# Loading, weight and summing order in a channel-gate kernel: a shorter lead load, a two-part first gate, and 16 rows of each tile summed on VectorE

## The chip, the cores and the metric

One core of one Trainium2 chip runs the program. The metric is the device time of one execution in microseconds (us). The kernel before took 528.62 us, the median of three runs (528.31 to 529.32). A profile's span, from the first to the last instruction, is about 1.5 us shorter than that time.

## The reference

```python
def reference(x, w1d):                      # x: 1 x 384 x 384 x 384 bf16, w1d: one bf16
    B, H, W, C = x.shape
    g = jnp.einsum("bhwc->bc", x) / (H * W)  # mean of every channel
    s = _sigmoid(g * w1d[0])                 # (cut: with k = 1 the padded loop is this product)
    return x * s[:, None, None, :]
```

Every element must be read once and written once, 113.25 MB each way. Only 384 channel sums stand between.

## The kernel before

The data are 1,152 rows of 128 partitions x 384 channels. Twelve rows are the lead, then 19 tiles of 60 rows follow through four slots of SBUF. The kernel guesses the gate from the first 4 rows (`s_early` in the code), multiplies each tile by that guess (VectorE; in place, but for the last tile, which goes to a free slot) and stores it. Meanwhile it sums all rows: TensorE 52 rows of each tile, VectorE 8. At the end it computes the true gate and compares the two bit by bit; if they differ, a second pass does everything again. On this input they agree, so the second pass never runs.

```python
FIRST, EARLY, TILE, SLOTS, BOTH, OWN, PAUSE = 12, 4, 60, 4, 3, 8, 8
...
    load(base, FIRST, 0)                                     # SyncE: the lead
    for k in range(BOTH):
        load(slot(k), TILE, row0(k), ("sync", "scalar"))     # half a tile on each queue
        if k == 0:
            plan.dma("scalar", w_one[0:1, 0:1], w1d.unsqueeze(0), writes=["w_one"])
    for k in range(BOTH, SLOTS):
        load(slot(k), TILE, row0(k))                         # tile 3: SyncE alone
...
    for k in range(n_tiles):
        if k >= SLOTS:
            for i in range(2) if k == SLOTS else () if k < SLOTS + 2 else (k - SLOTS,):
                sum_own(i)                                   # VectorE: 8 rows
                put(slot(i), TILE, row0(i))                  # gate in place, store on ScalarE
            if k == SLOTS:
                pause(slot(k))                               # ScalarE, after store 0 has landed
            load(slot(k), TILE, row0(k), reads=["pause"] if k == SLOTS else ())
...
    put(slot(last), TILE, row0(last), slot(n_tiles))         # last tile: gate, then own sum
    sum_own(last)
    put(base, FIRST, 0)
    join_own()                                               # then the true gate and the check
```

Because the gate works in place, it must wait until TensorE has read the rows. The load of tile k waits until the store of tile k - 4 has landed.

Of the kernel before, what the change touches and what calls it, by code (L numbers as in the profile page):

```python
# [149 lines left out]
def split(n, most):  # L150
    k = -(-n // most)
    return [n // k + (i < n % k) for i in range(k)]
# [3 lines left out]




FIRST, EARLY, TILE, SLOTS, BOTH, OWN, PAUSE = 12, 4, 60, 4, 3, 8, 8  # L160


def bass_standalone__channel_attn_eca__vision_kernel(
# [5 lines left out]
    B, H, W, C = x.shape  # L169
# [4 lines left out]
    def dram(view, r0, n):  # L174
        return view[r0 * P : (r0 + n) * P, :].rearrange("(p t) c -> p (t c)", p=P)

    ones = nc.alloc_sbuf_tensor("ones", [P, P], BF16)
    s_early = nc.alloc_sbuf_tensor("s_early", [P, C], BF16)
    w_one = nc.alloc_sbuf_tensor("w_one", [1, 16], BF16)
# [17 lines left out]
    def at(r0, n):  # L197
        assert r0 + n <= n_arena
        return arena[:, r0 * C : (r0 + n) * C]

    def rows(r0, n):
        return [("sb", r) for r in range(r0, r0 + n)]

    def gate(to, place, n, s):
        s_b = s[:].unsqueeze(1).broadcast_to([P, n, C])
        v, to_v = (at(r, n).rearrange("p (t c) -> p t c", t=n) for r in (place, to))
        return lambda e: e.tensor_tensor(to_v, v, s_b, ALU.mult)  # L207

    n_tiles = (n_rows - FIRST) // TILE
    base = SLOTS * TILE  # L210
# [3 lines left out]
    ready = nc.alloc_semaphore("ready")  # L214

    def slot(k):
        return k % SLOTS * TILE

    def row0(k):
        return FIRST + k * TILE  # L220
# [2 lines left out]
    s_true = at(base + FIRST, 1)  # L223
    plan = Planner(nc, "a", 70)

    def load(place, n, r0, queues=("sync",), reads=()):
        i = 0
        for queue, m in zip(queues, split(n, -(-n // len(queues)))):
            plan.dma(
                queue,  # L230
                at(place + i, m),
                dram(x_rows, r0, n)[:, i * C : (i + m) * C],
                reads=reads,
                writes=rows(place + i, m),
            )
            i += m
# [3 lines left out]
    def mm(e, bank, weights, moving, start, stop):  # L240
        if not loaded:
            loaded.append(e.matmul(bank, weights, moving, start=start, stop=stop))  # L242
            return loaded[0]
        return e.add_instruction(  # L244
            mybir.InstMatmult(
                name=nc.get_next_instruction_name(),
                engine=mybir.EngineType.PE,
                ins=[e.lower_ap(moving), e.lower_ap(weights)],
                outs=[e.lower_ap(bank)],
                start_tensor_calc=start,  # L250
                stop_tensor_calc=stop,
                ldweights=False,
            )
        )

    def add_rows(e, group, column, n, start, stop):

        n_wide = n * C // WIDE
        all_of = [
            mm(  # L260
                e,
                acc[group][i % 3][:, :],
                ones[:],
                arena[:, column + i * WIDE : column + (i + 1) * WIDE],
                start and i < 3,
                stop and i >= n_wide - 3,
            )
            for i in range(n_wide)
        ]
        return all_of[-1]  # L270
# [9 lines left out]
    def sum_others():  # L280

        def one(e, s):
            e.wait_ge(ready, 1).then_inc(ready, -1)  # L283
            add_rows(e, 1, slot(s) * C, TILE - OWN, False, False).then_inc(
                plan.sems["tensor"], 1
            )

        def emit(e):
            add_rows(e, 1, (base + EARLY) * C, 4, True, False)
            rounds = -(-n_tiles // SLOTS)  # L290
            some = n_tiles - (rounds - 1) * SLOTS
            with e.Fori(0, rounds) as k:
                for s in range(some):
                    one(e, s)
                if some < SLOTS:
                    with e.If(k < rounds - 1):
                        for s in range(some, SLOTS):
                            one(e, s)
            add_rows(
                e, 1, (base + EARLY + 4) * C, FIRST - EARLY - 4, False, True  # L300
            ).then_inc(plan.sems["tensor"], 1)

        plan.streams["tensor"].append(("block", emit, None))
# [16 lines left out]
    def sum_own(k):  # L320

        r0 = slot(k) + TILE - OWN
        view = at(r0, OWN).rearrange("p (t c) -> p c t", t=OWN)
        to = part if k else own
        plan.op(
            "vector",
            lambda e: e.reduce_sum(to[:], view, axis=mybir.AxisListType.X),  # L327
            reads=rows(r0, OWN),
            writes=["part" if k else "own"],
        )  # L330
        if k:
            plan.op(
                "vector",
                lambda e: e.tensor_tensor(own[:], own[:], part[:], ALU.add),  # L334
                reads=["own", "part"],
                writes=["own"],
            )
# [34 lines left out]
            writes=["total"],  # L372
        )

    def put(place, n, r0, to=None):
        to = place if to is None else to
        plan.op(
            "vector",
            gate(to, place, n, s_early),
            reads=["s_early"] + rows(place, n),  # L380
            writes=rows(to, n),
        )
        plan.final.append(
            plan.dma("scalar", dram(o_rows, r0, n), at(to, n), reads=rows(to, n))
        )

    def pause(r0):

        to = at(base + FIRST + 1, PAUSE)
        plan.op(  # L390
            "scalar",
            lambda e: e.activation(  # L392
                to, warm[:, 0:1].broadcast_to([P, PAUSE * C]), ACT_F.Sigmoid
            ),
            reads=["warm"],
            writes=rows(r0, 1) + ["pause"],
        )
# [26 lines left out]

    plan.op("gpsimd", lambda e: e.memset(warm[:, 0:1], 0.0), writes=["warm"])
    plan.op("vector", lambda e: e.memset(ones[:], 1.0), writes=["ones"])  # L426
    load(base, FIRST, 0)
    for k in range(BOTH):
        load(slot(k), TILE, row0(k), ("sync", "scalar"))
        if k == 0:  # L430
            plan.dma("scalar", w_one[0:1, 0:1], w1d.unsqueeze(0), writes=["w_one"])
    for k in range(BOTH, SLOTS):
        load(slot(k), TILE, row0(k))
    heads = {e: len(plan.streams[e]) for e in ("sync", "scalar")}
    weight()
    sum_first()
# [6 lines left out]
        reads=["total", "w_scaled0", "warm1"],  # L443
        writes=["s_early"],
    )
    plan.need("tensor", rows(base, FIRST))
    sum_others()

    for k in range(n_tiles):
        if k >= SLOTS:  # L450

            for i in range(2) if k == SLOTS else () if k < SLOTS + 2 else (k - SLOTS,):
                sum_own(i)
                put(slot(i), TILE, row0(i))
            if k == SLOTS:
                pause(slot(k))
            load(slot(k), TILE, row0(k), reads=["pause"] if k == SLOTS else ())
        there = rows(slot(k), TILE)
        plan.relay(ready, "gpsimd", "tensor", there, there, ["acc1"])
    plan.signals("tensor", rows(base, FIRST), ["acc1"])  # L460
    for k in range(n_tiles - SLOTS, last):
        sum_own(k)
        put(slot(k), TILE, row0(k))

    put(slot(last), TILE, row0(last), slot(n_tiles))
    sum_own(last)
    put(base, FIRST, 0)
# [9 lines left out]
        reads=["total", "w_scaled1"],  # L477
        writes=["s_true"],
# [6 lines left out]
        reads=["s_true", "s_early"],  # L485
        writes=["total"],
# [4 lines left out]
        reads=["total"],  # L491
        writes=["wrong"],
# [4 lines left out]
        reads=["wrong"],  # L497
        writes=["redo"],
# [5 lines left out]
    half, r0 = base // 2, 0  # L504
    for k, n in enumerate(split(n_rows, half)):
        place = k % 2 * half
# [4 lines left out]
            reads=rows(place, n),  # L511
            writes=rows(place, n),
# [9 lines left out]
    def ahead(name, e, n):  # L522




        block = nc.main_func.blocks[0].instructions
        at_end = len(block)
        plan.emit(name, e, n)
        new = block[at_end:]  # L530
        del block[at_end:]
        barrier = next(
            i
            for i, ins in enumerate(block)
            if ins.engine == e.engine and isinstance(ins, mybir.InstDrain)
        )
        block[barrier:barrier] = new

    ahead("sync", nc.sync, 1)
    ahead("scalar", nc.scalar, 1)  # L540
    plan.emit("sync", nc.sync, heads["sync"] - 1)
    plan.emit("scalar", nc.scalar, heads["scalar"] - 1)

    with nc.Block() as block:
# [66 lines left out]
```

## Time and profile before

| | before |
|---|---|
| time, median of 3 | 528.62 us |
| span of the profiled run | 527.0 us |
| bytes through the DMA engines | 226.51 MB |
| weight's matmul starts | 15.31 us |
| first tile's sum starts on TensorE | 24.18 us |
| first store issued / landed | 47.64 / 74.3 us |
| check ends / last store lands | 518.1 / 526.9 us |

VectorE idled for 73.6 us before its gates, waiting for TensorE. This is what the change goes at. No engine but the DMA engines is near its limit.

### The profile page before, as it was taken

The page shows a single profiled execution, that of the slowest core. Times are in us where ns is not written, and L with a number is a line of the kernel's source. Part 1 is how long each engine was busy: PE and PEld are TensorE (multiplying, and loading weights), DVE is VectorE, ACT ScalarE, POOL GpSimd, SP SyncE. Part 2 cuts the span into 40 slices and gives each one's busy share as a digit, 9 for nine tenths or more (in the row PEclk, how much of TensorE's full clock was granted, in tenths as well). Part 3 has the DMA queues.
Part 4 walks back from the last instruction along what each step waited for, and adds up shares of the span by engine and source line. Part 5 has one row for each costly group of instructions (what it writes and reads, how often), then busy time and mean ns, then how long its engine had stood idle before and what let it go on. Part 6 is the DMA issues. An engine that isn't in the chain of part 4 may idle for free. (4 is left out here: it accounts for less than half of the span.)

```text
span 527.0 us, 1015 instructions
## 1 busy us (share of the span) xinstructions
PE 198.5 (38%) x754; PEld 0.2 (0%) x2; DVE 353.9 (67%) x81; ACT 5.5 (1%) x5; POOL 0.3 (0%) x5
## 2 busy tenths in 40 slices
PE   0389170070706151524333342516060707070810
PEld 0000000000000000000000000000000000000000
DVE  0639999649494858576666666666666666758892
ACT  1000020000000000000000000000000000000000
POOL 0000000000000000000000000000000000000000
PEclk9999766576767667675758585858585858585765
DMA  9999999999999999999999999999999999999998
GB/s 383 434 421 418 448 448 395 444 448 448 395 444 448 448 395 444 448 444 399 444 448 444 399 444 448 445 399 444 444 444 406 441 444 444 406 441 444 444 406 363
DMA packets 6196, 226.51 MB, mean 430 GB/s; under 512 B 690, under 2 KB 690, under 8 KB 690
## 3 DMA queue, kind: packets, MB, share of 16 engines
q10 hardware_dynamic: 3314, 122.10, 53.6%
q1 hardware_dynamic: 2880, 104.40, 46.1%
q14 instruction: 2, 0.02, 0.0%
HBM read 113.25 MB, written 113.25 MB: 430 GB/s over the span
## 5 line engine op out<-in xcount | busy, mean ns | idle before, releaser
L244 PE MATMUL acc<-arena,ones 128*128 128x512 bf16 x749 | 196.6, 429 | 288.4 <-PEq L283 288.4
L207 DVE TENSOR_TENSOR arena<-arena,s_early 128x23040 bf16<-128x23040 bf16 (+1 forms) x20 | 233.5, 11677 | 78.0 <-PE acc L244 73.6
L327 DVE TENSOR_REDUCE part<-arena 128x384 f32<-128x3072 bf16 x18 | 96.4, 5355 | 67.3 <-DMA arena<-in_x_dram 67.3
L334 DVE TENSOR_TENSOR own<-own,part 128x384 f32<-128x384 f32 x18 | 10.0, 558 | 0.6
L418 DVE TENSOR_SCALAR w_scaled<-w_all 128x1 f32<-128x1 f32 x2 | 0.2, 152 | 14.3 <-PE w_all L409 14.3
L409 PE MATMUL w_all<-w_one,ones 1*128 1x1 bf16 x1 | 0.2, 158 | 15.3 <-DMA w_one<-in_w1d_dram 15.3
L244 PE MATMUL acc_own<-terms,ones 128*128 128x384 bf16 x3 | 1.4, 479 | 10.5 <-DVE terms L345 10.5
L327 DVE TENSOR_REDUCE own<-arena 128x384 f32<-128x3072 bf16 x1 | 5.3, 5305 | 0.0
L474 ACT ACTIVATE arena<-total,w_scaled 128x384 bf16<-128x384 f32 x1 | 0.6, 615 | 439.0 <-DVE total L315 439.0
L315 DVE TENSOR_TENSOR total<-total,acc 128x128 f32<-128x128 f32 (+2 forms) x11 | 4.5, 408 | 0.4
L392 ACT ACTIVATE arena<-warm 128x3072 bf16<-128x3072 f32 x1 | 2.8, 2763 | 54.1 <-DMA out_dram<-arena 54.1
L313 DVE COPY total<-acc 128x384 f32<-128x384 f32 x1 | 0.6, 558 | 1.2 <-PE acc L244 1.2
L403 ACT ACT_TABLE_LOAD x1 | 1.3, 1283 | 2.3 <-issue 2.3
L352 DVE TENSOR_TENSOR own<-own,terms 128x384 f32<-128x384 f32 x2 | 1.1, 558 | 0.1
L345 DVE CAST terms<-own 128x384 bf16<-128x384 f32 x3 | 1.1, 357 | 0.1
L482 DVE TENSOR_TENSOR total<-arena,s_early 128x384 f32<-128x384 uint16 x1 | 0.6, 557 | 0.7 <-ACT arena L474 0.7
L370 DVE TENSOR_TENSOR total<-total,acc_own 128x384 f32<-128x384 f32 x1 | 0.6, 554 | 0.6 <-PE acc_own L244 0.6
L426 DVE MEMSET ones<- 128x128 bf16 x1 | 0.2, 165 | 1.0 <-PEq L596 1.0
L440 ACT ACTIVATE s_early<-total,w_scaled 128x384 bf16<-128x384 f32 x1 | 0.6, 615 | 15.8 <-DVE total L315 15.8
L242 PE MATMUL acc<-arena,ones 128*128 128x512 bf16 x1 | 0.6, 608 | 0.0
L490 DVE TENSOR_REDUCE wrong<-total 128x1 f32<-128x384 f32 x1 | 0.6, 552 | 0.0
L403 ACT ACTIVATE warm<-warm 128x1 f32<-128x1 f32 x1 | 0.2, 203 | 0.0
(8 smaller groups left out, 0.9 us busy)
## 6 DMA issues: line engine op xcount, KB each, us to landing
out_dram<-arena ACTq DMA_DIRECT2D x19, 5760.0 KB, 47.4
arena<-in_x_dram SPq DMA_DIRECT2D x16, 5760.0 KB, 38.9
arena<-in_x_dram ACTq DMA_DIRECT2D x3, 2880.0 KB, 27.4
arena<-in_x_dram SPq DMA_DIRECT2D x3, 2880.0 KB, 36.4
arena<-in_x_dram SPq DMA_DIRECT2D x1, 1152.0 KB, 10.3
out_dram<-arena ACTq DMA_DIRECT2D x1, 1152.0 KB, 16.9
w_one<-in_w1d_dram ACTq DMA_DIRECT2D x1, 0.0 KB
```

What stands on the lines that cost most here:

```text
L207: return lambda e: e.tensor_tensor(to_v, v, s_b, ALU.mult)
L242: loaded.append(e.matmul(bank, weights, moving, start=start, stop=stop))
L244: return e.add_instruction(mybir.InstMatmult(name=nc.get_next_instruction_name(), engine=mybir.EngineType.PE, ins=[e.lower_ap(moving), e.l ...
L313: emit = lambda e, part=part, of=of: e.tensor_copy(part, of)
L315: emit = lambda e, part=part, of=of: e.tensor_tensor(part, part, of, ALU.add)
L327: lambda e: e.reduce_sum(to[:], view, axis=mybir.AxisListType.X),
L334: lambda e: e.tensor_tensor(own[:], own[:], part[:], ALU.add),
L345: lambda e, term=term: e.tensor_copy(term, own[:]),
L352: lambda e, term=term: e.tensor_tensor(own[:], own[:], term, ALU.subtract),
L370: lambda e: e.tensor_tensor(total[:], total[:], acc_own[:, :C], ALU.add),
L392: lambda e: e.activation(to, warm[:, 0:1].broadcast_to([P, PAUSE * C]), ACT_F.Sigmoid),
L403: lambda e: e.activation(warm[:, 1:2], warm[:, 0:1], ACT_F.Sigmoid),
```

## The change

Its intent is to make the first store earlier and to take TensorE's sum out of the gate's way. The lead is cut to 8 rows and the other 4 go to ScalarE's queue. The weight goes right behind the lead on SyncE's queue. The first tile is gated in two parts, of which the first needs only the first 32 rows summed. VectorE sums 16 rows of each tile in place of 8, TensorE 44 in place of 52. The pause on ScalarE becomes 9 rows long in place of 8.

```diff
-FIRST, EARLY, TILE, SLOTS, BOTH, OWN, PAUSE = 12, 4, 60, 4, 3, 8, 8
+FIRST, EARLY, TILE, SLOTS, BOTH, FORE, OWN = 12, 4, 60, 4, 3, 32, 16
+PAUSE = 9
...
-            add_rows(e, 1, slot(s) * C, TILE - OWN, False, False).then_inc(
-                plan.sems["tensor"], 1
-            )
+            for r, n in ((0, FORE), (FORE, TILE - OWN - FORE)):
+                add_rows(e, 1, (slot(s) + r) * C, n, False, False).then_inc(
+                    plan.sems["tensor"], 1
+                )
...
-    load(base, FIRST, 0)
-    for k in range(BOTH):
-        load(slot(k), TILE, row0(k), ("sync", "scalar"))
+    LEAD = EARLY + 4
+    load(base, FIRST, 0, hi=LEAD)
+    plan.dma("sync", w_one[0:1, 0:1], w1d.unsqueeze(0), writes=["w_one"])
+    for k in range(SLOTS):
+        load(slot(k), TILE, row0(k), ("sync", "scalar") if k < BOTH else ("sync",))
         if k == 0:
-            plan.dma("scalar", w_one[0:1, 0:1], w1d.unsqueeze(0), writes=["w_one"])
-    for k in range(BOTH, SLOTS):
-        load(slot(k), TILE, row0(k))
+            load(base, FIRST, 0, ("scalar",), lo=LEAD)
...
-                put(slot(i), TILE, row0(i))
+                put(slot(i), TILE, row0(i), parts=None if i else (FORE, TILE - FORE))
```

(Cut: `put` gates part by part, `load` takes a range of rows, the semaphores that tell of TensorE's parts, and the queue heads.)

More of the change, by code (lines that the diff above doesn't have):

```diff
@@ L224, in bass_standalone__channel_attn_eca__vision_kernel, with load @@
     plan = Planner(nc, "a", 70)
-    def load(place, n, r0, queues=("sync",), reads=()):
-        i = 0
-        for queue, m in zip(queues, split(n, -(-n // len(queues)))):
+    def load(place, n, r0, queues=("sync",), lo=0, hi=None, reads=()):
+        i, hi = lo, hi or n
+        for queue, m in zip(queues, split(hi - lo, -(-(hi - lo) // len(queues)))):
             plan.dma(
@@ L373, in join_own, with put @@
         )
-    def put(place, n, r0, to=None):
-        to = place if to is None else to
-        plan.op(
-            "vector",
-            gate(to, place, n, s_early),
-            reads=["s_early"] + rows(place, n),
-            writes=rows(to, n),
-        )
+    def put(place, n, r0, to=None, parts=None):
+        to, i = place if to is None else to, 0
+        for m in parts or [n]:
+            plan.op(
+                "vector",
+                gate(to + i, place + i, m, s_early),
+                reads=["s_early"] + rows(place + i, m),
+                writes=rows(to + i, m),
+            )
+            i += m
         plan.final.append(
@@ L445, in bass_standalone__channel_attn_eca__vision_kernel @@
     )
-    plan.need("tensor", rows(base, FIRST))
+    plan.need("tensor", rows(base, LEAD))
     sum_others()
@@ L457, in bass_standalone__channel_attn_eca__vision_kernel @@
             load(slot(k), TILE, row0(k), reads=["pause"] if k == SLOTS else ())
-        there = rows(slot(k), TILE)
-        plan.relay(ready, "gpsimd", "tensor", there, there, ["acc1"])
+        there = rows(slot(k), TILE) + (rows(base + LEAD, FIRST - LEAD) if k == 1 else [])
+        plan.relay(ready, "gpsimd", "tensor", there, rows(slot(k), FORE), ["acc1"])
+        plan.signals("tensor", rows(slot(k) + FORE, TILE - OWN - FORE), ["acc1"])
     plan.signals("tensor", rows(base, FIRST), ["acc1"])
@@ L537, in ahead @@
         block[barrier:barrier] = new
-    ahead("sync", nc.sync, 1)
+    ahead("sync", nc.sync, 2)
     ahead("scalar", nc.scalar, 1)
-    plan.emit("sync", nc.sync, heads["sync"] - 1)
+    plan.emit("sync", nc.sync, heads["sync"] - 2)
     plan.emit("scalar", nc.scalar, heads["scalar"] - 1)
```

## The prediction

> **What bounds the kernel now.** I read the page's slices first, then the windows, then the timeline of both ends, and last the waits of the DMA queues. The slices and the packet totals:
>
> ```profile
> DMA  9999999999999999999999999999999999999998
> GB/s 383 434 421 418 448 448 395 444 448 448 395 444 448 448 395 444 448 444 399 444 448 444 399 444 448 445 399 444 444 444 406 441 444 444 406 441 444 444 406 363
> DMA packets 6196, 226.51 MB, mean 430 GB/s; under 512 B 690, under 2 KB 690, under 8 KB 690
> ```
>
> The DMA engines are busy in every slice; VectorE is at 67% and TensorE at 38% of the span. The swing between 395 and 448 GB/s is no real swing: a slice counts a packet whole, and most packets are 46,080 bytes. Windows as long as one tile's period show it. The columns are the window, its length, busy time of PE, PEld, DVE, ACT and POOL, the granted clock, DMA share and GB/s:
>
> ```profile
> 408.00:435.20 27.20, 10.33 (x39) 0.00 (x0) 18.08 (x4) 0.00 (x0) 0.00 (x0) 0.69 1.00 434
> 435.20:462.40 27.20, 10.41 (x39) 0.00 (x0) 18.09 (x4) 0.00 (x0) 0.00 (x0) 0.69 1.00 434
> 462.40:489.50 27.10, 10.47 (x39) 0.00 (x0) 18.05 (x3) 0.00 (x0) 0.00 (x0) 0.69 1.01 435
> ```
>
> So the steady stage runs at 434 GB/s, with VectorE busy for 18.1 of 27.2 us. One row of the kernel is 128 x 384 x 2 = 98,304 bytes, which at 434 GB/s is 0.2265 us, or 4.415 rows per us. A tile is 60 rows in and 60 out, 27.2 us: the period is the traffic, nothing else. All 226.51 MB at 434 GB/s take 521.9 us. The span is 527.0 us, so only 5.1 us lie outside full-rate transfer, and no change that keeps the bytes can take more than that.
>
> I looked for those 5.1 us in the packet records, spreading each packet's bytes evenly over its own time. About 1.7 us are gone before the transfers are up to speed (first packet at 1.0 us). From 2 to 50 us, with loads alone, the rate is 430 to 433, which costs 0.4 us more. Between 50.6 and 53.5 us each of the 16 engines has one 46,080-byte load packet of about 2.6 us in place of 1.7 us, just ahead of the first store's first packet: 0.9 us. The steady stage adds 0.6 us of drift. The rest, some 1.5 us, is the tail: most engines finish their last data at 525.1 to 525.5, one at 526.46, and the final wait ends at 527.0.
>
> The head, with the work that the change touches:
>
> ```profile
> 15.31 0.16 PE L409 MATMUL w_all<-w_one,ones 1*128 1x1 bf16 x1 [15.31 <-DMA w_one<-in_w1d_dram]
> 19.52 5.30 DVE L327 TENSOR_REDUCE own<-arena 128x384 f32<-128x3072 bf16 x1
> 24.18 11.17 PE L244 MATMUL acc<-arena,ones 128*128 128x512 bf16 x39 [6.04 <-PEq L283]
> 35.45 12.16 DVE L207 TENSOR_TENSOR arena<-arena,s_early 128x23040 bf16<-128x23040 bf16 x1 [10.63 <-PE acc L244]
> 47.64 18.36 ACTq L109 DMA_DIRECT2D out_dram<-arena  x2
> ```
>
> The weight lands at 15.2, the first tile at 24.0, its TensorE sum ends at 35.4 and holds the gate, and the first store goes out at 47.64. That looks like a long latency, but 252 rows of loads need 252 x 0.2265 = 57 us, so the DMA engines have work throughout it. The queue's own waits and the issues say the same of the rest:
>
> ```profile
> SPq L109 <- DMA out_dram<-arena: 368.8, 14, 26.9
> out_dram<-arena ACTq DMA_DIRECT2D x19, 5760.0 KB, 47.4
> arena<-in_x_dram SPq DMA_DIRECT2D x16, 5760.0 KB, 38.9
> ```
>
> A store is in flight for 47.4 us and a load for 38.9 us, against a period of 27.2: on average 1.7 stores and 1.4 loads stand in the queues, and a load is never late for the engines, only for its slot.
>
> **What the Trainium skill says.** "DMA: Bandwidth & Descriptors", Specifications, gives a fabric ceiling of 435 GB/s; the 434 of the steady windows is that ceiling to within rounding. The same page, Queues, rings and completion order, says each engine takes packets in turn from the rings that have work. The trace agrees: in the head, packets of q1 (SyncE) and q10 (ScalarE) alternate one for one on each engine, so a small packet costs the other ring nearly nothing, and a transfer's landing depends on what it alternates with. "VectorE: DVE Perf Modes", the perf-mode tier table, lists tensor_reduce at one element per cycle only. The trace has 3,072 elements in 5.36 us, 1.74 ns each, even slower, so the page bounds this cost only from below. "TensorE: Matmul & The Clock Gate", Part 1, gives half clock until some microseconds of activity have passed; in the trace the first tile's matmuls start 427 ns apart for 13 of them and then 216 ns apart.
>
> **The change, part by part.** *Lead of 8 rows.* Its 8 packets per engine are 6,144 bytes in place of 9,216. ScalarE's first packets start only at 2.7 us, so about 6 of the 8 pass alone and the lead lands near 6 us (10.3 before). *Weight on SyncE.* It is next on that ring, one or two turns of 0.85 us later: about 7.6 us (15.2 before). From the weight to s_early took 20.24 - 15.31 = 4.9 us, so s_early stands at about 12.5. *Rows 8 to 11 on ScalarE.* While SyncE's half of tile 0 moves, its partner packets are partly these 3,072-byte ones, not 23,040-byte ones of tile 1. In total 8 + 60 + about 4 rows precede the landing: 72 x 0.2265 = 16.3, plus the 1.9 us of start, so about 18 us (24.0 before).
>
> *VectorE 16 rows.* The reduce is 6,144 elements: 10.7 us if time goes with the elements, about 8.5 us if part of the 5.36 us belongs to each of the 384 outputs (one cycle per element plus 5.2 cycles an output). I take 10.7 to be safe. In the first tile it starts when ScalarE's half lands, about 14.5, and ends by 25. *TensorE 44 rows.* 33 matmuls a tile in place of 39. The first 32 rows are 24 matmuls: 13 x 0.427 + 11 x 0.216 = 7.9 us, so from 18.2 to 26.1. *Gate in two parts.* 12.16 us for 60 rows is 0.203 us a row: 6.5 us for 32 rows, 5.7 us for 28, together 12.2 with almost no added cost. It begins at 26.1 and ends at 38.3. The first store goes out at about 38.5, 9 us earlier.
>
> What these 9 us buy is little. At 38.5 ScalarE's ring still has loads until about 42, so the store queues behind them and starts then, not at 53. Store 0 lands at about 70 (74 before), then the pause (9 rows: 9/8 x 2.76 = 3.1 us), and load 4 goes out at about 73 (77 before). VectorE then needs 10.7 + 0.56 + 12.16 = 23.4 us a tile (18.1 before): stores 1, 2 and 3 at about 62, 85 and 108 (65.7, 83.5, 101.4 before). They are needed where the store before them ends, about 70, 92 and 120. Both rings stay filled, and 23.4 is under 27.2. The ceiling is the same.
>
> At the end, the own sum of the last tile adds 5.3 us to the path of the last store and of the check, less the 4 us by which the loads run earlier:
>
> ```profile
> 510.01 0.34 ACTq L109 DMA_DIRECT2D out_dram<-arena  x1
> 517.94 0.15 DVE L496 CAST redo<-wrong 128x1 int32<-128x1 f32 x1
> ```
>
> The last store would be issued at about 511.5 and is needed when the 60 rows before it are through, about 523. The check would end near 519.5 and its flag is read in 1.8 us; the stores end at about 525. Both stay hidden.
>
> The sum: traffic 521.9 unchanged; start 1.7 unchanged; read-only drift shorter by about 0.1; the 0.9 us pause of the engines before the first store gone or not, I give it 50%, so 0.45; tail unchanged. 528.62 - 0.1 - 0.45 is 528.1 us.
>
> **The rivals.** *First: the pause before the first store goes away wholly.* It may come from ScalarE's ring starting again after it ran dry at 41; in the changed kernel it does not run dry. For it: no such gap is seen where a ring stays filled. Against: SyncE's ring runs dry at 69 and starts again at 77 without a loss, so it may belong to the first write to HBM, which remains. If it goes: 527.6. *Second: VectorE becomes the bound.* This needs a 16-row reduce over 27.2 - 12.7 = 14.5 us, 2.4 ns an element. Nothing in the trace speaks for it; 18 reduces lie within 5.29 to 5.43 us. If it came, 1 us over would cost about 15 us: 540 and more. *Third: a ring runs dry* in the head, because stores 2 and 3 come 2 to 7 us later than before, or at the end. My margins are 7 to 12 us; a miss would cost 1 to 3 us: 530. *Fourth: the latency is worth its face value*, 9 us, 519. The windows contradict it, as 521.9 is the floor.
>
> **Range and chances.** Rivals one and four bound it from below at about 527; repeats before spread from 528.31 to 529.32, and a short dry ring costs about 1. So 526.9 to 529.2. Over 2% faster would be below 518, under the floor: 1%. Over 2% slower needs the second rival: 2%.
>
> **What would show it.** Right: weight matmul near 8, first tile's matmuls near 18, gates of 6.5 and 5.7 us, first store near 38.5, reduces of 8.5 to 10.7 us, 434 GB/s in a steady window. The pause shows in the packets just before the first store. Wrong: VectorE without idle time before its reduces in the steady stage, or a window of a tile's length under 430 GB/s.

## More of the kernel before

The slices, the steady windows, both ends of the timeline and the queue's waits stand in the prediction. Two more views are needed for the comparison. These are the page's line of busy time by engine, two groups of instructions (line, engine, operation, tiles and shapes, count, then busy us and mean ns, then idle time before them), and one DMA issue line (count, size, us to landing):

```profile
PE 198.5 (38%) x754; PEld 0.2 (0%) x2; DVE 353.9 (67%) x81; ACT 5.5 (1%) x5; POOL 0.3 (0%) x5
...
L207 DVE TENSOR_TENSOR arena<-arena,s_early 128x23040 bf16<-128x23040 bf16 (+1 forms) x20 | 233.5, 11677 | 78.0 <-PE acc L244 73.6
L327 DVE TENSOR_REDUCE part<-arena 128x384 f32<-128x3072 bf16 x18 | 96.4, 5355 | 67.3 <-DMA arena<-in_x_dram 67.3
...
arena<-in_x_dram ACTq DMA_DIRECT2D x3, 2880.0 KB, 27.4
```

## The result

The changed kernel took 528.29 us, the median of 6 runs (528.18 to 528.51); in the same rounds the kernel before took 529.16 us in its 6 (528.31 to 530.3). The ratio is 0.9984, with a 95% interval of 0.9971 to 0.9997. Ratios here are the mean time of one kernel's runs over that of the other's runs of the same rounds, so not quite the ratio of the medians.

The slices and packets of the changed kernel, then its windows of a tile's period (columns as in the prediction):

```profile
DMA  9999999999999999999999999999999999999998
GB/s 387 430 422 460 406 448 395 444 448 448 395 444 448 448 395 444 448 441 402 444 448 434 409 445 444 434 413 441 448 430 416 441 444 434 416 441 444 430 420 367
DMA packets 6340, 226.51 MB, mean 430 GB/s; under 512 B 706, under 2 KB 706, under 8 KB 962
```

```profile
408.00:435.20 27.20, 9.10 (x33) 0.00 (x0) 23.18 (x3) 0.00 (x0) 0.00 (x0) 0.69 1.00 434
435.20:462.40 27.20, 9.17 (x33) 0.00 (x0) 23.18 (x3) 0.00 (x0) 0.00 (x0) 0.69 1.00 434
```

The bytes and the rate are the same to the last digit that is shown. VectorE went from 18.1 to 23.2 us of a 27.2 us period, and the rate did not change. The page's busy line, the two groups and the DMA issues say where its work went:

```profile
PE 178.2 (34%) x640; PEld 0.2 (0%) x2; DVE 451.1 (86%) x82; ACT 5.8 (1%) x5; POOL 0.3 (0%) x5
...
L209 DVE TENSOR_TENSOR arena<-arena,s_early 128x23040 bf16<-128x23040 bf16 (+3 forms) x21 | 233.5, 11123 | 5.2 <-DMA arena<-in_x_dram 4.0
L331 DVE TENSOR_REDUCE part<-arena 128x384 f32<-128x6144 bf16 x18 | 189.5, 10526 | 53.4 <-DMA arena<-in_x_dram 53.4
...
out_dram<-arena ACTq DMA_DIRECT2D x19, 5760.0 KB, 44.7
arena<-in_x_dram SPq DMA_DIRECT2D x16, 5760.0 KB, 40.9
arena<-in_x_dram ACTq DMA_DIRECT2D x3, 2880.0 KB, 34.5
```

The gates' wait for TensorE fell from 73.6 us to nearly none, and the reduces doubled in its place. ScalarE's three half-tile loads take 34.5 us to land (the median, so the middle one), not 27.4. That line turns out to matter. The head of the changed kernel's timeline:

```profile
9.18 0.16 PE L415 MATMUL w_all<-w_one,ones 1*128 1x1 bf16 x1 [9.18 <-DMA w_one<-in_w1d_dram]
...
14.56 10.49 DVE L331 TENSOR_REDUCE own<-arena 128x384 f32<-128x6144 bf16 x1 [1.08 <-DMA arena<-in_x_dram]
...
26.31 12.23 DVE L209 TENSOR_TENSOR arena<-arena,s_early 128x12288 bf16<-128x12288 bf16 x2 [1.26 <-PE acc L247]
...
38.57 23.45 ACTq L109 DMA_DIRECT2D out_dram<-arena  x2
...
74.23 3.08 ACT L398 ACTIVATE arena<-warm 128x3456 bf16<-128x3456 f32 x1 [60.11 <-DMA out_dram<-arena]
```

The first store is issued at 38.57 us, 9.1 us earlier than before. But the pause behind its landing starts at 74.23, where it started at 74.31 before: the whole 9 us were lost in the queue. In the packet records, ScalarE's ring (its queue on each of the 16 DMA engines) still carries loads. Their last packet ends at 51.0 us and the load lands at 53.2 us. The first store's first packet starts at 51.3 us on one engine and at 54.7 to 55.2 on the others. Before, it came at 53.1 to 53.5. So load 4 is issued at 77.34 (77.10 before), and from there on the two kernels run the same course. The tail:

```profile
502.05 10.41 DVE L331 TENSOR_REDUCE part<-arena 128x384 f32<-128x6144 bf16 x1
...
515.55 0.34 ACTq L109 DMA_DIRECT2D out_dram<-arena  x1
...
523.48 0.15 DVE L503 CAST redo<-wrong 128x1 int32<-128x1 f32 x1
```

The check ends at 523.6 us, 5.5 us later than before. ScalarE then reads the flag and passes its waits for the stores; it is through all but the last at 526.07 us, and the last store lands at 526.67. The room between the two was 6 us before (waits through at 520.8, last landing at 526.9) and is down to 0.6 us.

### The profile page after: what moved, and what is told of

The parts are those of the page before. It is cut to its first block, busy times and chain, and to the rows that moved or that the text cites. A ratio compares the mean times of both kernels' runs of the same rounds, so it can differ in the third digit from the quotient of the medians. Undisturbed runs are those within 1.5% of the kernel's fastest.

```text
span 526.7 us, 905 instructions
## 1 busy us (share of the span) xinstructions
PE 178.2 (34%) x640; PEld 0.2 (0%) x2; DVE 451.1 (86%) x82; ACT 5.8 (1%) x5; POOL 0.3 (0%) x5
## 4 chain that ended last, share of the span: by engine, by line
DMA 64%; DVE 27%; issue 4%; PE 2%; ACT 0%; DVEq 0%
DMA out_dram<-arena 33%; DMA arena<-in_x_dram 31%; DVE arena L209 13%; DVE part L331 12%; PE acc L247 1%; DVE own L338 1%; DVE total L319 0%; DVE own L356 0%; DVE terms L349 0%; ACT arena L481 0%; DVE total L489 0%; DVE total L374 0%; DVE wrong L497 0%; PE acc_own L247 0%; DVE redo L503 0%
## 5 line engine op out<-in xcount | busy, mean ns | idle before, releaser
L247 PE MATMUL acc<-arena,ones 128*128 128x512 bf16 x635 | 176.3, 447 | 314.0 <-PEq L286 314.0
L209 DVE TENSOR_TENSOR arena<-arena,s_early 128x23040 bf16<-128x23040 bf16 (+3 forms) x21 | 233.5, 11123 | 5.2 <-DMA arena<-in_x_dram 4.0
L331 DVE TENSOR_REDUCE part<-arena 128x384 f32<-128x6144 bf16 x18 | 189.5, 10526 | 53.4 <-DMA arena<-in_x_dram 53.4
L331 DVE TENSOR_REDUCE own<-arena 128x384 f32<-128x6144 bf16 x1 | 10.5, 10495 | 1.1 <-DMA arena<-in_x_dram 1.1
L398 ACT ACTIVATE arena<-warm 128x3456 bf16<-128x3456 f32 x1 | 3.1, 3082 | 60.1 <-DMA out_dram<-arena 60.1
L245 PE MATMUL acc<-arena,ones 128*128 128x512 bf16 x1 | 0.6, 608 | 0.0
## 6 DMA issues: line engine op xcount, KB each, us to landing
arena<-in_x_dram ACTq DMA_DIRECT2D x3, 2880.0 KB, 34.5
```

The costliest lines, as they stand in the source:

```text
L209: return lambda e: e.tensor_tensor(to_v, v, s_b, ALU.mult)
L245: loaded.append(e.matmul(bank, weights, moving, start=start, stop=stop))
L247: return e.add_instruction(mybir.InstMatmult(name=nc.get_next_instruction_name(), engine=mybir.EngineType.PE, ins=[e.lower_ap(moving), e.l ...
L331: lambda e: e.reduce_sum(to[:], view, axis=mybir.AxisListType.X),
L398: lambda e: e.activation(to, warm[:, 0:1].broadcast_to([P, PAUSE * C]), ACT_F.Sigmoid),
```

## The experiments

The questions are these. Is the difference of 0.16% real, and which part makes it? What are the 0.9 us before the first store? How close are the two other bounds, the tail and VectorE? And where do the long runs of the kernel before come from? Twelve runs were made, all with correct results.

### Before against itself, the change again, and its halves

These four ran on one chip in the same rounds, five of them. The first is unchanged:

> The kernel before, unchanged, timed against itself. Both theories: ratio 1.000; the width of the interval says how small a difference can be believed. If the spread of the first six runs (528.31 to 530.3) is of the kernel, its runs should again spread over 1 to 2 us, and its profile should show one DMA engine ending 1 us or more after the others.

The change again:

> The changed kernel again. Theory A (the transfers alone set the time, the change moves only what lies under them): within 0.5 us of before in the median, ratio 0.998 to 1.000. Theory B (the earlier first store buys real time): ratio below 0.9975, and the gain shows as bytes moved earlier in the head, which the first profile does not have (the lag behind full rate at 70 us was 3.1 us before and 3.1 us after).

The order of loads without the larger sum:

```diff
-FIRST, EARLY, TILE, SLOTS, BOTH, FORE, OWN = 12, 4, 60, 4, 3, 32, 16
+FIRST, EARLY, TILE, SLOTS, BOTH, FORE, OWN = 12, 4, 60, 4, 3, 32, 8
```

> The changed kernel with 8 rows of each tile on VectorE as before, so only the load order, the weight's queue, the two-part gate and the pause remain. Theory A: 528 to 529 us, ratio 0.998 to 1.001; the first store later than 38.6 us by some 1 us because TensorE's sum of tile 0 has 39 matmuls, no matter. The check at the end is back at about 518 us, away from the end. Theory B: at least as fast as the whole change, by 1 us.

The larger sum alone, on the kernel before:

```diff
-FIRST, EARLY, TILE, SLOTS, BOTH, OWN, PAUSE = 12, 4, 60, 4, 3, 8, 8
+FIRST, EARLY, TILE, SLOTS, BOTH, OWN, PAUSE = 12, 4, 60, 4, 3, 16, 8
```

> The kernel before with 16 rows of each tile on VectorE and nothing else. Theory A: 528 to 529.5 us, ratio 0.999 to 1.002; reduces of 10.5 us, VectorE busy for 23.3 us of a period of 27.2, check at the end near 523.5 us in place of 518.1. Theory B, as far as the balance of the engines matters: ratio under 0.9975.

| run | median us | lowest to highest | ratio to before, 95% interval |
|---|---|---|---|
| before, of these rounds | 528.92 | 528.16 to 531.68 (11 runs) | |
| before against itself | 529.76 | 528.44 to 531.97 | 1.0017 (0.9985 to 1.005) |
| the change again | 528.20 | 528.12 to 528.54 | 0.9978 (0.9954 to 1.0003) |
| load order alone | 528.65 | 528.18 to 529.98 | 0.9991 (0.9965 to 1.0018) |
| larger sum alone | 530.45 | 528.80 to 534.82 | 1.0044 (0.9999 to 1.0088) |

The lowest runs of the two kernels are 528.16 and 528.12 us: in an undisturbed run the change is worth nothing that can be seen. The ratio under 1 comes from the long runs that the kernel before had and the changed kernel did not have in its 12 runs: counting all runs of these rounds and the first ones, 12 of 23 of the kernel before are over 529 us, and 0 of 12 of the changed kernel. Whether the change prevents the long runs or met none by luck is open. Each half alone still has them (529.98 and 534.82 us), and so do two kernels below that add only a small write to the changed kernel. The kernel before against itself has an interval from 0.9985 to 1.005, so a difference of 0.2% is not shown by such rounds. As expected its runs again spread widely (3.5 us), and in its profile the latest DMA engine ended its last packet 1.3 us after the middle of the 16. The load order alone behaves as the transfers' theory says (its check is back at 518.1 us). Its first store goes out at 38.39, no later than with the whole change. That was a miss of my expectation: the two-part gate needs only the first 32 rows in either case.

The larger sum alone is a miss in size: I had expected up to 529.5 us. The interval of its ratio just includes 1, so that it is slower is not shown by the times alone. Its trace (a run of 529.75, span 528.2) tells why. The last load lands at 492.11, not 489.5, and the check ends late:

```profile
525.63 0.15 DVE L496 CAST redo<-wrong 128x1 int32<-128x1 f32 x1
```

The last store landed at 527.15, but ScalarE passed its last wait only at 528.24. In this run the end is no longer set by the transfers but by the work behind the last load. From its landing to the end it took 528.24 - 492.11 = 36.1 us; in the changed kernel the same stretch is 526.07 - 489.95 = 36.1 us.

### A longer run of the larger sum, in a trace

> One more look at the kernel before with 16 rows on VectorE, whose six runs spread from 528.8 to 534.8 us, to catch a long run in a trace. Theory T (exposed tail): the end is the last load's landing plus 36.1 us (gate, own sum, base gate, join, check, flag, waits), so a run of 533 us has its last load landing near 496 us and ScalarE's final waits after the last landing. Theory S (one slow DMA engine): the last data packet of one engine ends several us after the others. Theory I (idle rings in the head): the lag behind full rate at 150 us is several us over 3.2.

It took 530.86 us (span 529.4). The last load landed at 493.20 and the waits ended at 529.36, again 36.2 us. So the tail's theory (Theory T) holds. The run also was slower before the tail. The last data packets of the 16 engines ended between 524.8 and 527.9 us, where in the changed kernel all but two ended within 524.8 to 525.4. And the engines' lag (the time by which the bytes moved so far trail a steady 434 GB/s) was 0.8 us larger at 100 us than at 70. So two things came together in this run, slow engines and the exposed tail. Why the last load lands 2.6 to 3.7 us later than in the kernel before, though its loads have the same order, was not settled. Slow engines are not enough for it: at 480 us the lag of these two traces was only 0.1 and 0.5 us larger than in the kernel before.

### More rows on VectorE

> The changed kernel with 20 rows of each tile on VectorE and 40 on TensorE. Theory T (beside the transfers, the end has a second bound: the last load's landing plus the work after it): that work is 36.1 us with 16 rows and 0.658 us a row more, so 38.7 us here; with the last load landing at about 490 us the final waits end at 528.7 in place of 526.7: 530.3 us, ratio about 1.003 over the kernel before. VectorE needs 25.9 us a tile, under the period of 27.2, so nothing changes before the tail. Against it, transfers alone: 528.3.

The edit is the same line with 20 in place of 16. It measured 529.84 us (529.61 to 530.48), ratio 1.0024 (1.0007 to 1.0041). The last load landed at 490.27 and the waits ended at 528.98, that is 38.7 us, as expected to the tenth; the last store had landed at 526.99. The span is 529.0, expected 528.7. Its steady window, and then its last reduce in the timeline:

```profile
408.00:435.20 27.20, 9.13 (x30) 0.00 (x0) 25.73 (x3) 0.00 (x0) 0.00 (x0) 0.63 1.00 434
```

```profile
502.37 12.97 DVE L331 TENSOR_REDUCE part<-arena 128x384 f32<-128x7680 bf16 x1
```

The steady stage still runs at 434 GB/s with VectorE busy 25.7 of 27.2 us, so the extra 2.3 us of span come from the tail. The changed kernel stands just short of this edge.

> The changed kernel with 24 rows of each tile on VectorE and 36 on TensorE. VectorE needs 24 x 0.658 + 0.56 + 12.15 = 28.5 us a tile, over the period of 27.2, so it becomes the bound: from 14.6 us on, 19 tiles x 28.5 = 541.5 us, then 2.5 + 8 + 2.5 us of base gate, join, check and flag: span about 569 us, time about 570. Transfers alone: 528.3.

The same line with 24, in one look: 564.45 us, span 562.9. The groups of VectorE show no idle time before the reduces:

```profile
L331 DVE TENSOR_REDUCE part<-arena 128x384 f32<-128x9216 bf16 x18 | 281.2, 15624 | 0.0
```

A window as long as one tile's turn on VectorE, 28.2 us, has it busy throughout and the transfers under their rate:

```profile
408.00:436.20 28.20, 7.35 (x27) 0.00 (x0) 28.17 (x4) 0.00 (x0) 0.00 (x0) 0.62 1.01 423
```

VectorE is the bound, as expected. My 569 us were 6 too many: the reduce takes 15.62 us, not 15.8, and instructions in a row overlap a little, so tiles follow each other every 28.22 us and not every 28.5 (19 x 0.28 = 5.3 us). The four sizes of reduce, 5.36, 10.53, 13.06 and 15.62 us for 8, 16, 20 and 24 rows, lie on a line of 0.64 us a row.

### The 0.9 us before the first store

A small write to the output, first on ScalarE's queue; the last store overwrites it and waits for it:

```diff
+    plan.dma(
+        "scalar", dram(o_rows, 0, 1)[:, :P], dram(x_rows, 0, 1)[:, :P], writes=["early"]
+    )
     load(base, FIRST, 0, hi=LEAD)
```

> The changed kernel with a small write to HBM (256 bytes of each of 128 rows, copied from the input, overwritten by the last store) put first on ScalarE's queue. Theory F (the 0.7 to 0.9 us stretch of one load packet on every engine just ahead of the first store belongs to the first write to HBM): the stretch is gone at 52 us, and since this write runs while the engines are only starting, the lag behind full rate at 70 us falls from 3.0 to about 2.2 us and the time to about 527.5 us, ratio to before about 0.996. Theory G (the stretch belongs to the first 46,080-byte store, or to the turn from loads to stores): the stretch stays at 52 us, 528.3 us.

It measured 531.20 us (528.66 to 532.77; ratio to the kernel before 1.0059, 1.0038 to 1.0079): 0.6% slower, which neither theory foresaw. The changed kernel itself did not run in these rounds, so what the small write alone costs is not measured. In its trace (the run of 528.66) no load packet is stretched ahead of the first store any more. But between 4 and 10 us the engines lost 0.8 us they had not lost before, with stretched packets just behind the small write. The loss moved and was not hidden.

The second form of the write reads from SBUF and stands in the middle of the loads:

```diff
             load(base, FIRST, 0, ("scalar",), lo=LEAD)
+            plan.dma("scalar", dram(o_rows, 0, 1)[:, :P], ones[:], reads=["ones"], writes=["early"])
```

> The changed kernel with a small write to HBM from SBUF (256 bytes of each of 128 partitions, overwritten by the last store) put on ScalarE's ring in the middle of the loads, so that it runs near 18 to 22 us. Theory F: the stretch moves there: about 0.7 us lost near 20 us, none at 52 us, time unchanged at 528.3. Theory G: nothing near 20 us, the stretch stays at 52 us.

It measured 529.49 us (528.14 to 531.06; ratio 1.0026, 1.0005 to 1.0047). Here the small write cost the 16 engines together nothing that can be seen in 18 to 30 us, and the stretch stayed just ahead of the first store (load packets of 1.1 to 1.4 us in place of 0.86, at 58 to 59 us; 0.6 us in all). So the first theory gets one run for it and one against it. What the stretch belongs to is open; that it is worth no more than 0.9 us is not. The second form shows one thing more, on which the account of the prediction below rests. The small write is 32 KB, which at 434 GB/s is 0.08 us, but it is 8 packets of 256 bytes on each engine, and they pass from 21.1 to 28.0 us, one for about each 0.86 us packet of SyncE. ScalarE's last half tile then lands at 60.5 us in place of 53.2, and its loads take longer in the issue line:

```profile
arena<-in_x_dram ACTq DMA_DIRECT2D x3, 2880.0 KB, 44.1
```

Both kernels with the small write have long runs though the kernel before did not on that chip (528.32 to 528.94 in 7 runs). Both have 16 rows on VectorE, so they have the thin tail of the changed kernel, but no long run of theirs was caught in a trace; that cause is argued, not shown.

### Looking for a long run of the kernel before

> One more look at the kernel before, whose runs spread from 528.2 to 532.0 us. In a long run: Theory S gives one DMA engine that ends 2 to 4 us after the others; Theory I a lag over 4 us at 150 us; Theory T is out here, as the check ends 9 us before the last landing.

> One more look at the kernel before, to catch one of its long runs (531 to 532 us) in a trace. Theory S (slow DMA engines): the last packets of the 16 engines end over 2 to 5 us, as in the longer run of the 16-row version of the kernel before. Theory I (idle rings in the head): a lag over 4 us at 150 us. A run of 528.2 to 528.9 tells nothing.

> The same once more: Theory S gives ends of the engines spread over 2 to 5 us in a long run, Theory I a lag over 4 us at 150 us; a short run tells nothing.

They took 528.55, 528.54 and 528.37 us, on two other chips: no long run was caught. So these runs tell nothing of the long ones. In all three the latest engine's last packet came 1.1 us or more after the middle of the 16, as in the first profile (1.2). The long runs of 530 to 532 us, seen on one chip and once in the first rounds, stay unexplained.

## Why the prediction was right

The time, 528.29 us, is 0.2 us over the 528.1 predicted and inside the range.

**The bound held.** The steady windows are at 434 GB/s in every kernel here but the one that VectorE bounds, and the bytes did not change. 521.9 us of the 526.7 us of span remain transfer at full rate.

**The head's steps.** The lead landed at 7.7 us (near 6 predicted), the weight at 9.0 (7.6), s_early stood at 14.1 (12.5), tile 0 landed at 18.5 (18), ScalarE's half at 14.5 (14.5), TensorE's first 32 rows let the gate go at 26.3 (26.1), and the first store went out at 38.57 (38.5). The early misses of about 1.5 us had no effect, since the half tile's landing at 14.5 came after them. Their source is a misreading: I let 6 of the lead's 8 packets on each engine pass before ScalarE's first packet at 2.7 us, but in the trace 3.4 had on average (2.2 in the kernel before).

**The step that failed** is "ScalarE's ring still has loads until about 42, so the store queues behind them and starts then, not at 53". Its load packets last until 51.0 us, and the store starts near 55. I had counted rows and forgotten turns. The engines alternate packet by packet, so while ScalarE's ring sends its 3,072-byte packets against SyncE's 23,040-byte ones, it moves hardly anything: 38 to 69 GB/s in the stretches of 2 us between 14 and 22 us, while SyncE's ring has 360 to 392. At 22 us the ring has moved 34 rows, where it had moved 49 before. The rest of its loads therefore comes later, from 46 us on beside tile 3's packets of 46,080 bytes (133 and then 68 GB/s for ScalarE's ring), and its last half tile lands at 53.2 us where it landed at 42.6 before. The 34.5 us in the issue line show the same of the middle half tile. That turns and not bytes count is confirmed by the small write among the loads: 8 more packets per engine of almost no bytes moved this landing to 60.5 us. A second part of the miss is smaller: behind its last load packet, which ended at 50.6 to 51.0 us on 15 engines, ScalarE's ring moved nothing on them for some 4 us, though the store had been queued since 38.57. Why is open. With it falls "Store 0 lands at about 70" (74.2), "load 4 goes out at about 73" (77.3), and the 4 us that I took off the tail. The check ended at 523.6 and not near 519.5, and the room at the end was 0.6 us and not the 3 to 4 that my numbers gave. The conclusion survived by that margin, no more; to that extent it was luck.

**The work of VectorE.** The reduce is 10.53 us, near the 10.7 that I took to be safe; 8.5 was the wrong model. The two gates took 12.23 us together (12.2). A tile is 23.2 us (23.4).

**The coin toss.** I gave the 0.9 us pause before the first store 50% to vanish, and with it 0.45 us. It stayed, at 0.7 us. So the number came out within 0.2 us although a credit of 0.45 in it was not paid: part of that closeness is luck. The first rival is refuted in its condition: ScalarE's ring did not run dry, and the stretch came all the same.

**The other rivals.** VectorE became the bound at 24 rows and not at 16 or 20, which fits the prediction's limit of 14.5 us for the reduce (13.06 passed, 15.62 did not). A dry ring did not show. The latency's face value of 9 us was worth nothing.

## What to carry to other kernels

When the DMA engines are full from end to end, an earlier first store is only an earlier place in a queue: ask when the ring ahead of it empties, and count turns and not bytes, since a ring of small packets falls behind one of large packets. Work moved onto an idle engine is free only until the tail, where it lies between the last load and the end; add up that path as well as the steady period, and keep room for a late last load. Time the kernel against itself before believing a few tenths of a per cent.

## What the Trainium skill lacked or had wrong

- "DMA: Bandwidth & Descriptors", Queues, rings and completion order, tells of turns by packet, but not what follows when two rings' packets differ in size: a ring with packets of 3,072 bytes beside one of 23,040 got 38 to 69 GB/s of 430 for 8 us, and its later transfers landed 11 us later.
- "VectorE: DVE Perf Modes", the perf-mode tier table, gives tensor_reduce one element per cycle. With neighbours 768 bytes apart (384 bf16), each further row of 384 elements took 0.64 us, 1.67 ns an element, between 3,072 and 9,216 elements (the whole reduces took 1.74 to 1.70 ns an element). "SBUF — State Buffer" (the note on 16-byte cachelines) says that crossing lines costs a penalty, without a number.
- No page that I read has the stretch of a load packet on every engine ahead of the first store: 0.3 to 0.9 us once per execution, in every kernel traced but the one with the small write first. What it belongs to is open.
- "DMA: Bandwidth & Descriptors", Latency and other measured facts, calls two of the engines usually slower and lays it, as a guess, to the descriptor rings of GpSimd's queue. No transfer here comes from that queue, and still one or more engines lag: with nearly equal bytes (about 14.16 MB each), the latest of 16 ended 1.2 us after the middle in the first profile, and it alone sets the last landing; in the changed kernel two ended 0.9 and 1.1 us after it. The records don't name the engine.
